# One PSUM bank for two or four groups of a feed-forward's first layer

## The chip, the cores and the metric

The kernel runs on one core of a Trainium2 chip. The metric is device time in microseconds, the median of three runs. Five instruction streams matter: PE (TensorE, matmuls and transposes; PEld is its weight load), DVE (VectorE), ACT (ScalarE), POOL (GpSimd) and SP, which issues nearly all DMAs. Each works through its own queue in order and waits for the others by semaphores.

## The reference

Eight batches of eight heads go through an attention in which each query keeps only its 32 largest scores. The heads are joined to rows of 512, and these go through a feed-forward layer with an ELU.

```python
# q, k, v: (8, 8, 576, 64); w_in: (512, 2048); w_out: (2048, 512)
scores = scale * np.matmul(q, k.transpose(0, 1, 3, 2))
kth = np.partition(scores, -32, axis=-1)[..., -32:-31]
scores = np.where(scores >= kth, scores, -1e9)
attn = np.exp(scores - max) / (sum + 1e-9)
x = (attn @ v) transposed and joined to (4608, 512)
h = x @ w_in
g = np.where(h > 0, h, np.exp(np.minimum(h, 0)) - 1)
out = g @ w_out
```

The kernel computes g as relu(h) + exp(-relu(-h)) - 1. The weights arrive as 64-bit floats, and the kernel turns them into 32-bit floats itself.

## The kernel before

**Attention.** The work is cut into 144 steps. A step is 128 query rows of a pair of heads (or 64 rows of four heads, for the 64 rows that are left of 576). `scores` (L301 on PE, L309 on ACT) forms 2 x 576 scores per row. `select` (L343, L348, L355 on DVE; in the first eight steps `select_row` with L320, L324, L330) finds the 32 largest of each with four rounds of an eight-fold maximum (MAX8) and three replacements between them. `mask` takes the threshold and the maximum on POOL (L368 neg, L370 gap) and masks and exponentiates on ACT (L371, L372). `normalise` forms the reciprocal of the sum and scales the rows on POOL (L382 to L389). `turn` transposes them on PE (L408, tiles eps and scps) with copies on ACT (L409, tile et), and `attend` multiplies by v (L434); ACT copies the result to xT (L461).

**Feed-forward.** Finished rows are gathered in blocks of one, two or three slots of 128 tokens: in the first two batches five blocks of one slot and two of two, and in each later pair of batches three of two slots and one of three. `ffn_pieces(blk)` cuts a block's work into pieces. `hidden(f)`, for f = 0 to 15, is one group: four matmuls (L502) that give 128 hidden units of all tokens of the block in a PSUM tile hps, whose pool `ps_f` has two buffers of one bank (512 fp32 per partition). A fp32 matmul leaves two records in the profile. ACT reads each group twice, relu(-h) to n (L510) and relu(h) to gT (L511). After each second group ACT takes exp(-n) (L513) of both, and a gate is noted. The gate, `close_gates` (L478), is the DVE instruction that forms gT + n - 1. `project` is the second layer, in four parts of four matmuls per slot (L523, tile ops, from the same pool `ps_f`), a copy (L532) and a DMA out.

**Order.** `feed` is called four times a step and takes pieces from the list as their costs and due times allow. It closes a gate at the second feeding place after that in which it was noted. A new pair of groups and `project` may close gates earlier. From step eight on (`tight`) the order of PE, ACT, DVE and POOL is that in which the code names the instructions (`manual_schedule`). In the first eight steps a scheduler orders them. There the 32 weight blocks are also converted, two or three between the rounds of a row (`hook`): three operations on ACT (L170, L171, L172), a clamp on POOL (L173), two on DVE (L180, L183) and an addition on POOL (L187). All hidden groups of the first one-slot block fall into these eight steps too.

Of the kernel before, what the change touches and what calls it, by code (L numbers as in the profile page):

```python
# [8 lines left out]
AF = mybir.ActivationFunctionType  # L9
ALU = mybir.AluOpType  # L10
FP32 = mybir.dt.float32
# [69 lines left out]
def kernel(  # L81
# [9 lines left out]
    nc = tc.nc  # L91
    P = nc.NUM_PARTITIONS
    B, H, S, D = q.shape
    dm, dff = moe_w_in.shape[0], moe_w_in.shape[1] // 2
# [7 lines left out]
    NG = NF // 2  # L102
    T = 3 * P
    KEYS, QUERIES = R, R + S
    scale = 1.0 / float(D) ** 0.5
# [3 lines left out]
    def pool(name, bufs, **kw):  # L109
        return ctx.enter_context(tc.tile_pool(name=name, bufs=bufs, **kw))  # L110
# [12 lines left out]
    ps_f = pool("ps_f", 2, space=PSUM)  # L123
    wide = [ps_sc.tile([P, 2, JP], FP32, tag=f"s{i}", name="scps") for i in range(2)]
    late = {}
    raws = ExitStack()
    early = raws.enter_context(tc.tile_pool(name="early", bufs=1))
    earlyf = raws.enter_context(tc.tile_pool(name="earlyf", bufs=2))
# [326 lines left out]
    def finish(blk, parts, at, cols, src):  # L455
        if blk.xT is None:
            if blk.slots == 1:
                blk.xT = xpool.tile([P, NC, P], FP32, tag="xT", name="xT")
            else:
                blk.xT = late["x"].tile([P, NC, T], FP32, tag="xT", name="xT")  # L460
        nc.scalar.copy(blk.xT[:, at, cols], src)  # L461
        blk.left -= parts
        if blk.left == 0:
            ffn.extend(ffn_pieces(blk))

    gates = []
    place = [0]

    def close_gates(keep=0, upto=None):

        while gates:
            put, group, dst, n = gates[0]
            if put > place[0] - keep if upto is None else group > upto:
                return
            gates.pop(0)
            nc.vector.scalar_tensor_tensor(  # L478
                out=dst, in0=n, scalar=-1.0, in1=dst, op0=ALU.add, op1=ALU.add
            )  # L480

    def ffn_pieces(blk):
        n_tok = blk.slots * P

        def hidden(f):
            if f == 0 and blk.number == 0:
                g = early.tile([P, NF, P], FP32, tag="g", name="gT")
                blk.gT = [g[:, 0:NG], g[:, NG:NF]]
            elif f % NG == 0 and blk.number > 0:
                g = late["g"].tile([P, NG, T], FP32, tag="g", name="gT")  # L490
                blk.gT.append(g[:])
            if f % 2 == 0:
                if len(gates) > 1:
                    close_gates(upto=gates[0][1])
                if blk.number == 0:
                    n = earlyf.tile([P, 2, P], FP32, tag="n", name="n")
                else:
                    n = late["f"].tile([P, 2, T], FP32, tag="n", name="n")
                blk.n = n[:, :, 0:n_tok]
            ps = ps_f.tile([P, dm], FP32, tag="f", name="hps")  # L500
            for i in range(NC):
                nc.tensor.matmul(  # L502
                    ps[:, 0:n_tok],
                    w_in[:, i, f * P : (f + 1) * P],
                    blk.xT[:, i, 0:n_tok],
                    start=(i == 0),
                    stop=(i == NC - 1),
                )
            g = blk.gT[f // NG]
            nc.scalar.activation(blk.n[:, f % 2, :], ps[:, 0:n_tok], AF.Relu, scale=-1.0)  # L510
            nc.scalar.activation(g[:, f % NG, 0:n_tok], ps[:, 0:n_tok], AF.Relu)  # L511
            if f % 2 == 1:
                nc.scalar.activation(blk.n, blk.n, AF.Exp, scale=-1.0)  # L513
                dst = g[:, f % NG - 1 : f % NG + 1, 0:n_tok]
                gates.append((place[0], (blk.number, f - 1), dst, blk.n))

        def project(s, part):
            close_gates(upto=(blk.number, (part + 1) * NF // 4 - 1))
            if part == 0:
                blk.o = ps_f.tile([P, dm], FP32, tag="f", name="ops")  # L520
            step = NF // 4
            for f in range(part * step, (part + 1) * step):
                nc.tensor.matmul(  # L523
                    blk.o[:],
                    blk.gT[f // NG][:, f % NG, s * P : (s + 1) * P],
                    w_out[:, f, :],
                    start=(f == 0),
                    stop=(f == NF - 1),
                )
            if part == 3:  # L530
                o = opool.tile([P, dm], FP32, tag="osb", name="osb")
                nc.scalar.copy(o[:], blk.o[:])  # L532
                for t in blk.tiles[s]:
                    p0 = t.cols.start - s * P
                    nc.sync.dma_start(out[t.rows, :], o[p0 : p0 + t.ql, :])

        part = HIDDEN[blk.slots]
        behind = 2 * NF if blk.number else 0
        return [
            (part, max(behind, NC * (f // 4 + 1)), lambda f=f: hidden(f))  # L540
            for f in range(NF)
        ] + [
            (PROJECT, max(behind, NF + (part + 1) * NF // 4),
             lambda s=s, part=part: project(s, part))
            for s in range(blk.slots)
            for part in range(4)
        ]
# [4 lines left out]
    for b in range(B):  # L552
        if b % 2 == 0:
# [5 lines left out]
            for part in division:  # L559
                blk = Block(len(blocks), len(part))  # L560
# [4 lines left out]
        for qt in range(J + 1):  # L565
# [8 lines left out]
            t = Tile(b, qt, rows, blk, slice(c0, c0 + n))  # L574
# [6 lines left out]
        for qts in order:  # L581
# [3 lines left out]
            for qt in qts:  # L585
                n = len(steps)
# [12 lines left out]
    for b in range(1, B):  # L599
        f = first[b]  # L600
# [137 lines left out]
```

## Time and profile before

| | us |
|---|---|
| median of three runs (1681.44 to 1681.5) | 1681.44 |
| the profiled execution, whole time | 1682.55 |
| the profiled execution, first to last instruction (span) | 1680.8 |
| PE busy | 1604.5 |
| DVE busy | 1534.4 |
| ACT busy | 1167.5 |
| POOL busy | 638.8 |
| mean granted TensorE clock | 0.971 |

The profile is one execution of the program. Times within it count from its first instruction. Line numbers (L502) are those of the kernel file. A row of the groups has engine, operation, tiles (written <- read), shapes and count, then busy time with the mean duration of one in ns, then the idle time of that engine just before and what ended it. A line of waits reads "engine, tile, line <- what it waited for: us in total, times, longest".

### The profile page before, as it was taken

How to read it: one execution, taken by the hardware profiler on the slowest of the kernel's cores; microseconds unless marked ns; L12 is line 12 of the kernel's file. 1: busy time of each engine (PE TensorE's matmuls, PEld its weight loads, DVE VectorE, ACT ScalarE, POOL GpSimd, SP SyncE). 2: the span in 40 equal slices, each digit the busy share in tenths (PEclk: the TensorE clock that was granted, in tenths of full speed). 3: DMA queues.
4: the chain of work that ended last, by engine and by line, in shares of the span. 5: the costliest groups of instructions: out<-in, count | busy, mean ns of one | idle time of the engine just before them, and what ended most of it. 6: DMA issues, size and time to landing. Idle time of an engine off the chain costs nothing.

```text
span 1680.8 us, 26396 instructions
## 1 busy us (share of the span) xinstructions
PE 1604.5 (95%) x8560; PEld 1041.7 (62%) x8560; DVE 1534.4 (91%) x3096; ACT 1167.5 (69%) x2661; POOL 638.8 (38%) x1719
## 2 busy tenths in 40 slices
PE   6767999999999999999999999999999999999999
PEld 4554776667575666656557575756558575755565
DVE  6999999999999999999999999999998999998600
ACT  6776786778776776767768685857758586857531
POOL 3776333433333334434334333333333333332200
PEclk8567999999999999999999999999999999999999
DMA  7441021001200111001200111001100000000000
GB/s 192 134 156 39 16 56 36 7 1 47 52 7 7 29 35 42 1 21 36 49 14 1 36 35 42 1 13 43 43 13 8 21 21 29 7 7 7 7 13 13
DMA packets 101129, 56.22 MB, mean 33 GB/s; under 512 B 84097, under 2 KB 92289, under 8 KB 100993
## 3 DMA queue, kind: packets, MB, share of 16 engines
q1 hardware_dynamic: 99792, 54.26, 11.6%
q8 instruction: 68, 1.11, 0.3%
q14 instruction: 69, 0.56, 0.1%
q10 hardware_dynamic: 1200, 0.30, 0.1%
HBM read 45.09 MB, written 9.44 MB: 32 GB/s over the span
## 4 chain that ended last, share of the span: by engine, by line
PE 59%; DVE 26%; ACT 5%; issue 1%; POOL 1%; ACTq 0%; DVEq 0%; POOLq 0%
PE ops L523 22%; PE hps L502 19%; DVE wk L348 11%; DVE m L355 9%; PE avps L434 7%; PE scps L301 6%; PE eps L408 4%; DVE m L343 3%; DVE gT L478 2%; ACT sc L372 1%; ACT sc L371 1%; PE qkps L271 1%; ACT et L409 1%; PE scps L408 1%; ACT n L510 0%
## 5 line engine op out<-in xcount | busy, mean ns | idle before, releaser
L502 PE MATMUL hps<-xT,w_in 128*128 128x256 f32 (+2 forms) x2432 | 557.4, 378 | 25.9 <-ACT gT L511 23.6
L355 DVE MAX8 m<-wk 128x8 f32<-128x576 f32 x816 | 574.5, 744 | 0.0
L523 PE MATMUL ops<-w_out,gT 128*128 128x512 f32 x1152 | 523.8, 599 | 0.0
L502 PEld LDWEIGHTS hps<-xT,w_in 128*128 128x128 f32 x2432 | 411.5, 195 | 127.4 <-ACT gT L511 34.4
L348 DVE MATCH_REPLACE8 wk<-m,wk 128x576 f32<-128x576 f32 x544 | 399.2, 740 | 0.0
L523 PEld LDWEIGHTS ops<-w_out,gT 128*128 128x128 f32 x1152 | 209.0, 190 | 233.6 <-issue 218.7
L382 POOL TENSOR_SCALAR dene<-den 128x2 f32<-128x2 f32 x144 | 34.8, 242 | 832.9 <-ACT sc L372 832.7
L371 ACT ACTIVATE sc<-sc,neg 128x576 f32<-128x576 f32 x288 | 226.4, 786 | 63.2 <-POOL neg L368 63.0
L372 ACT ACTIVATE sc<-sc,gap 128x576 f32<-128x576 f32 x288 | 223.2, 775 | 25.2
L309 ACT ACTIVATE sc<-scps 128x576 f32<-128x576 f32 x288 | 173.6, 662 | 76.6 <-PE scps L301 76.6
L389 POOL TENSOR_SCALAR sc<-sc,rec 128x576 f32<-128x576 f32 x288 | 219.5, 773 | 15.2 <-POOL rec L387 0.6
L409 ACT COPY et<-eps 128x512 f32<-128x512 f32 x288 | 167.5, 582 | 68.4 <-PE eps L408 68.2
L301 PE MATMUL scps<-kqT 64*128 64x288 f32 (+1 forms) x1280 | 200.5, 439 | 15.1 <-ACT kqT L277 8.3
L348 DVE MATCH_REPLACE8 wk<-m,sc 128x576 f32<-128x576 f32 x272 | 199.6, 740 | 0.0
L408 PEld LDWEIGHTS eps<-ident,sc 128*128 128x128 f32 x1152 | 145.1, 145 | 82.9 <-issue 48.0
L478 DVE SCALAR_TENSOR_TENSOR gT<-n,gT 128x512 f32<-128x512 f32 (+2 forms) x152 | 106.5, 701 | 97.7 <-ACT n L513 97.6
L434 PE MATMUL avps<-et,vT 128*64 128x256 f32 (+2 forms) x2080 | 190.4, 326 | 2.7 <-ACT et L409 2.3
L343 DVE MAX8 m<-sc 128x8 f32<-128x576 f32 x272 | 191.0, 742 | 0.0
L408 PE MATMUL eps<-ident,sc 128*128 128x128 f32 x1152 | 178.1, 281 | 12.9 <-POOL sc L389 11.9
L510 ACT ACTIVATE n<-hps 128x256 f32<-128x256 f32 (+2 forms) x304 | 112.6, 370 | 85.5 <-PE hps L502 75.0
L434 PEld LDWEIGHTS avps<-et,vT 128*64 128x64 f32 x2080 | 123.5, 141 | 73.1 <-issue 24.2
L301 PEld LDWEIGHTS scps<-kqT 64*128 64x128 f32 (+1 forms) x1280 | 107.7, 181 | 83.6 <-issue 44.8
(47 smaller groups left out, 1226.8 us busy)
## 6 DMA issues: line engine op xcount, KB each, us to landing
kin<-in_k_dram SPq DMA_DIRECT2D x64, 128.0 KB, 2.8
raw<-in_moe_w_in_dram SPq DMA_DIRECT2D x16, 512.0 KB, 4.4
vT<-in_v_dram SPq DMA_DIRECT2D x64, 128.0 KB, 2.3
raw<-in_moe_w_out_dram SPq DMA_DIRECT2D x16, 512.0 KB, 3.2
out_dram<-osb SPq DMA_DIRECT2D x32, 256.0 KB, 2.3
qin<-in_q_dram SPq DMA_DIRECT2D x62, 128.0 KB, 2.8
kin<-in_k_dram SPq DMA_DIRECT2D x32, 32.0 KB, 2.5
vT<-in_v_dram SPq DMA_DIRECT2D x64, 16.0 KB, 2.2
```

Source lines behind the costliest of these rows:

```text
L301: nc.tensor.matmul(wide[i][rows, half, 0:HS], kq[part, q0 : q0 + u.t.ql], kq[part, k0 : k0 + HS], start=True, stop=True,)
L343: nc.vector.max(found[i], cur[i])
L348: nc.vector.match_replace(wk[i], found[i], cur[i], TAKEN)
L355: nc.vector.max(found[i], cur[i])
L371: nc.scalar.activation(sc, sc, AF.Prelu, bias=neg[:], alpha=STEEP)
L372: nc.scalar.activation(sc, sc, AF.Exp, bias=gap[:], accum_out=u.den[:, i : i + 1])
L389: nc.gpsimd.tensor_scalar(u.sc[:, i, :], u.sc[:, i, :], rec[:, i : i + 1], 1.0, ALU.mult, ALU.mult)
L408: nc.tensor.transpose(ps[:, c * P : (c + 1) * P], sc[:, c0 : c0 + P], ident[:])
L409: nc.scalar.copy(g.et[:, chunks, u.at, :], ps[:, 0 : n * P].rearrange("p (c q) -> p c q", c=n),)
L434: nc.tensor.matmul(ps[i * D : (i + 1) * D, cols], vt[:, 2 * J + i if c == J else i * J + c, :], w, start=(c == 0), stop=(c == J),)
L502: nc.tensor.matmul(ps[:, 0:n_tok], w_in[:, i, f * P : (f + 1) * P], blk.xT[:, i, 0:n_tok], start=(i == 0), stop=(i == NC - 1),)
L523: nc.tensor.matmul(blk.o[:], blk.gT[f // NG][:, f % NG, s * P : (s + 1) * P], w_out[:, f, :], start=(f == 0), stop=(f == NF - 1),)
```

## The change

The hps tile of a block of one slot now holds four groups (4 x 128 columns), that of two slots two groups (2 x 256), and that of three slots one group, as before (384). ACT reads relu(-h) and relu(h) of the whole bank in one instruction each, after the last of its groups. The unit for which exp and gate are issued is four groups for one slot (512 columns, before 256) and two for two and three slots, as before (512 and 768). The matmuls are the same, and so are the pieces, their costs and their due times. The tile n is addressed without gaps. The line numbers of what follows move by up to eight: the matmul is L506, the reads L516 and L519, exp L521, and the second layer's matmul L531 in the changed file.

```diff
     def ffn_pieces(blk):
         n_tok = blk.slots * P
+        bank = dm // n_tok
+        unit = max(2, bank)
...
-            if f % 2 == 0:
+            if f % unit == 0:
                 if len(gates) > 1:
                     close_gates(upto=gates[0][1])
                 if blk.number == 0:
-                    n = earlyf.tile([P, 2, P], FP32, tag="n", name="n")
+                    n = earlyf.tile([P, 4 * P], FP32, tag="n", name="n")
                 else:
-                    n = late["f"].tile([P, 2, T], FP32, tag="n", name="n")
-                blk.n = n[:, :, 0:n_tok]
-            ps = ps_f.tile([P, dm], FP32, tag="f", name="hps")
+                    n = late["f"].tile([P, 2 * T], FP32, tag="n", name="n")
+                blk.n = n[:, 0 : unit * n_tok].rearrange("p (f t) -> p f t", f=unit)
+            if f % bank == 0:
+                ps = ps_f.tile([P, dm], FP32, tag="f", name="hps")
+                blk.h = ps[:, 0 : bank * n_tok].rearrange("p (f t) -> p f t", f=bank)
             for i in range(NC):
                 nc.tensor.matmul(
-                    ps[:, 0:n_tok],
+                    blk.h[:, f % bank, :],
                     w_in[:, i, f * P : (f + 1) * P],
...
-            g = blk.gT[f // NG]
-            nc.scalar.activation(blk.n[:, f % 2, :], ps[:, 0:n_tok], AF.Relu, scale=-1.0)
-            nc.scalar.activation(g[:, f % NG, 0:n_tok], ps[:, 0:n_tok], AF.Relu)
-            if f % 2 == 1:
+            g, end = blk.gT[f // NG], f % NG + 1
+            if end % bank == 0:
+                n0 = f % unit + 1 - bank
+                nc.scalar.activation(
+                    blk.n[:, n0 : n0 + bank, :], blk.h, AF.Relu, scale=-1.0
+                )
+                nc.scalar.activation(g[:, end - bank : end, 0:n_tok], blk.h, AF.Relu)
+            if end % unit == 0:
                 nc.scalar.activation(blk.n, blk.n, AF.Exp, scale=-1.0)
-                dst = g[:, f % NG - 1 : f % NG + 1, 0:n_tok]
-                gates.append((place[0], (blk.number, f - 1), dst, blk.n))
+                dst = g[:, end - unit : end, 0:n_tok]
+                gates.append((place[0], (blk.number, f + 1 - unit), dst, blk.n))
```

## The prediction

> **What bounds the kernel now.** The page comes first, since it says which engines can be the limit at all.
>
> ```profile
> PE 1604.5 (95%) x8560; PEld 1041.7 (62%) x8560; DVE 1534.4 (91%) x3096; ACT 1167.5 (69%) x2661; POOL 638.8 (38%) x1719
> ```
>
> Two engines are nearly full, PE and DVE. The change takes work mainly from ACT, which is not. So the question is which of the two is the limit where. The busy times by stage answer that (columns: length, then PE, PEld, DVE, ACT, POOL with their instructions, the granted TensorE clock, DMA):
>
> ```profile
> 0.00:42.00 42.00, 26.18 (x111) 17.07 (x112) 28.52 (x59) 26.78 (x53) 14.19 (x42) 0.83 0.70 192
> 42.00:148.00 106.00, 78.19 (x361) 57.48 (x361) 100.28 (x172) 85.38 (x191) 79.86 (x116) 0.65 0.41 131
> 148.00:300.00 152.00, 136.69 (x1091) 99.89 (x1090) 150.50 (x319) 107.26 (x288) 57.81 (x166) 0.98 0.12 30
> 300.00:717.00 417.00, 407.22 (x2291) 273.56 (x2289) 416.34 (x858) 310.45 (x726) 162.17 (x467) 1.00 0.09 23
> 717.00:1600.00 883.00, 879.44 (x4452) 547.20 (x4451) 833.20 (x1685) 618.26 (x1360) 322.76 (x926) 1.00 0.08 22
> 1600.00:1681.00 81.00, 76.73 (x265) 46.51 (x262) 5.54 (x8) 19.33 (x49) 2.04 (x5) 0.99 0.04 13
> ```
>
> From 42 to 717 us DVE lacks only 5.7 + 1.5 + 0.7 us of being full: DVE sets the pace. From 717 us PE lacks 3.6 of 883 us and then 4.3 at the very end: PE sets the pace. The chain of waits, cut to 300 to 717 us, agrees: it is DVE's.
>
> ```profile
> by line: DVE wk L348 42.3%; DVE m L355 35.6%; DVE m L343 12.6%; DVE gT L478 5.7%; issue 2.8%; ACT sc L372 0.4%; ACT sc L371 0.4%; ACT et L409 0.2%; ACT n L513 0.2%; POOL neg L368 0.1%; DVEq L478 0.0%; ACTq L372 0.0%
> ```
>
> Which waits could end? Those of DVE and, apart from them, the one of PE that the change addresses:
>
> ```profile
> DVE gT L478 <- ACT n L513: 97.6, 28, 44.1
> DVE raw L180 <- POOL raw L173: 19.1, 6, 9.7
> ```
>
> ```profile
> PE hps L502 <- ACT gT L511: 23.6, 23, 4.0
> ```
>
> All 23.6 us of the last lie before 717 us (10.0 in 42:148, 9.4 in 148:300, 4.2 in 300:717). There PE has spare time and DVE has none, so ending them gives nothing by itself. Of DVE's 97.6 us only 2.1 lie before 717 us (1.43 at 283 us, 0.66 at 487 us); the rest is DVE waiting for a full PE. Of DVE's 19.1 us on the weight conversion, 5.7 lie in 42:148.
>
> **The change, part by part.** Time is won only where DVE, before 717 us, gets shorter or waits less. A microsecond won there moves everything behind it, because the order of PE's, DVE's and SP's work after 148 us is the same in both programs apart from the gates (L478), whose number falls.
>
> ```profile
> L478 DVE SCALAR_TENSOR_TENSOR gT<-n,gT 128x512 f32<-128x512 f32 x88 | 63.9, 726 | 83.7 <-ACT n L513 83.7
> ...
> L478 DVE SCALAR_TENSOR_TENSOR gT<-n,gT 128x256 f32<-128x256 f32 x40 | 19.0, 476 | 1.4 <-ACT n L513 1.4
> ```
>
> *DVE gates.* The five one-slot blocks had 40 gates of 256 columns and get 20 of 512; those of the other blocks keep number and size. In the chain a 256-wide gate costs 0.32 us and a 512-wide one 0.59. After 148 us: 32 x 0.32 = 10.2 becomes 16 x 0.59 = 9.4, so -0.8. Before 148 us eight gates took 5.3 us, three of them over 1.0; less 0.07 overlap each, 4.7. Four of 512 with one or two held up come to 3.1: -1.6. Here the Trainium skill speaks against: "SBUF — State Buffer", section "Who interferes with whom", says that a DVE instruction with two SBUF inputs contends with a GpSimd instruction that reads SBUF. A gate is one, and a longer one meets POOL more easily. If each of the 20 waited for one 1.3 us POOL addition, the loss would be 26 us and the gates a cost. The rows say otherwise: 476 ns against 400 unhindered is 0.08 per gate, 726 against about 660 is 0.07. The hold-up goes by the gate, not by its length, and there are fewer. I take -2.4 for both stages.
>
> *ACT.* Rows:
>
> ```profile
> L409 ACT COPY et<-eps 128x512 f32<-128x512 f32 x288 | 167.5, 582 | 68.4 <-PE eps L408 68.2
> ...
> L510 ACT ACTIVATE n<-hps 128x256 f32<-128x256 f32 x176 | 67.3, 382 | 46.9 <-PE hps L502 41.2 <-DVE m L355 3.1 <-DVE gT L478 2.6
> L513 ACT ACTIVATE n<-n 128x512 f32<-128x512 f32 x88 | 56.5, 642 | 0.0
> ...
> L510 ACT ACTIVATE n<-hps 128x128 f32<-128x128 f32 x80 | 21.9, 273 | 11.1 <-PE hps L502 6.4 <-DVE gT L478 3.6
> ```
>
> No 512-wide Relu exists; the 512-wide copy out of PSUM (0.58) is the nearest row, and 0.38 to 0.49 from 256 to 384 columns gives 0.59. Two-slot blocks: 352 reads of 0.383 = 135 us become 176 of 0.59 = 104. One-slot: 160 of 0.275 = 44 become 40 of 0.59 = 24, and 40 Exp of 0.423 become 20 of 0.642 (-4). ACT loses 55 us of busy time. None of it counts, as ACT is not the limit. What counts is when the Exp that frees a gate ends. After the last matmul of a two-slot unit there were 0.38 + 0.38 + 0.64 = 1.4 us; now 0.59 + 0.59 + 0.64 = 1.8: 0.4 us later.
>
> The Trainium skill speaks against this part too: "PSUM — Partial Sum Buffer", "Summary: rules for kernel authors", says to read another bank than the one that a matmul writes. So nothing of a bank may be read before its last group is written. That holds the first read back by one two-slot group (8 matmul records x 0.216 = 1.7 us) or three one-slot groups (24 x 0.131 = 3.1 us); 20 one-slot units x 3.1 would be 63 us if DVE stood waiting. In the trace it does not: a gate stands two feeding places behind its last group and waited twice before 717 us. The gate waits for the last group's Exp either way, so the price is 0.4 us at those gates that have no slack. That is the one at 487 us: +0.4. The 1.43 at 283 us stood behind a PE wait for ACT (1.01 us just before) of the kind that two banks of four groups relieve: -1.4 (0 to -1.4). PE's waits for a bank should nearly vanish after 148 us, at no gain.
>
> *The first stage.* Here the order is not written by hand, and the changed program's order differs on all engines. I followed it by hand with the durations of the trace. The stall to explain first, POOL's rows and then DVE's:
>
> ```profile
> 104.29 0.23 POOL L382 TENSOR_SCALAR dene<-den 128x2 f32<-128x2 f32 x1 [1.71 <-ACT sc L372]
> ...
> 108.40 0.75 POOL L389 TENSOR_SCALAR sc<-sc,rec 128x576 f32<-128x576 f32 x1
> 109.24 0.61 POOL L173 TENSOR_SCALAR raw<-raw 128x512 f32<-128x512 f32 x1
> ```
>
> ```profile
> 105.68 0.74 DVE L324 MATCH_REPLACE8 wk<-m,wk 128x576 f32<-128x576 f32 x1
> 109.88 1.51 DVE L180 TENSOR_SCALAR raw<-raw 128x512 uint32<-128x512 uint32 x1 [3.46 <-POOL raw L173]
> ```
>
> The 21st weight's clamp (L173) stands behind a whole normalisation on POOL's queue, and DVE behind the clamp. In the changed order this clamp comes before the normalisation; the 22nd comes behind it. On the other side PE now issues 13 first-layer matmuls in one piece (26 records x 0.26 = 6.8 us, from about 82 to 89 us, and 8 more records), ahead of the transposes (eps) that started at 88.2. ACT's copies of these, and the conversions queued behind them, come later: the 18th by 4 us, the 19th by 2. DVE then stands about 2.1 us at the 19th, where it did not, 1.8 at the 22nd, and 0.45 and 0.9 where it had 1.64 and 0.31: 5.3 in place of 5.7, or -0.4. The conversion that followed the stall at 109.88 ran 1.51 us beside POOL where an unhindered one takes 0.40: -1.1 if it runs free (0 to -1.1; I take -0.8). By the end of this stage: -1.2 besides the gates, with a hand count that may be off by 4 us either way.
>
> *After 717 us* PE's work is unchanged, and it has no idle time to give. 0, bounded by -1 (part of its 3.6 us) and +3 (ACT's longer burst in front of a copy that PE needs). The end is 64 + 128 matmul records back to back: 0.
>
> Sum: gates -2.4, first stage -1.2, wait at 283 us -1.4, wait at 487 us +0.4: -4.6. The profiled span of 1680.8 becomes 1676.2. That execution took 1682.55 in all, and the median of the runs is 1681.44, 0.64 above the span; so about 1676.8.
>
> **The rivals.** A: as summed, 1672 to 1678. B: the first stage gives nothing and the 283 us wait stays: only gates, -2.4 + 0.4, 1679.4. The many reorderings speak for it. It also covers the case in which the change loosens PE's 23.6 us and nothing else, and that in which DVE, 18 times waiting for Exp in 717:1600, hands some of the 0.4 us on. C: the conversion stalls go altogether (-5.7 instead of -0.4): 1671.5. For it speaks the lighter ACT; against it, the normalisation on POOL's queue stays. D, slower: the single-piece bursts on PE. Units two and three of block 0 are issued as 20 and 16 matmuls in one piece, where the first has 13: 3 to 7 x 0.52 = 1.6 to 3.6 us more. If each delays transposes, ACT's in-order queue and a clamp as the first does, DVE stands 3.7 and 5.7 us: +9.4 - 4.6, about 1686.2. It decides from the point where a burst outlasts the roughly 3.4 us that DVE takes from one conversion to the next. Against it: the slow clock (0.65) rises by then, and these bursts stand where fewer conversions queue behind them.
>
> **How the numbers follow.** A 55% (47 faster, 8 same), B 22% (2 faster, 20 same), C 8% (faster), D 15% (13 slower, 2 same). The bound for "same" is 0.2%, or 3.4 us, about what a measurement of this kernel can tell from no change. Faster 0.57, same 0.30, slower 0.13. The range reaches from C less a little, 1670, to the border of D, 1684.
>
> **What would show it.** Right: 20 gates of 512 more and 40 of 256 fewer; ACT near 1112 us busy; Relu at 0.59; PE's wait hps <- ACT under 10 us; DVE's row at 1534 less 3 to 5; the stage after 717 us as long as before. Wrong: new DVE idle before gates in 148:717; more than 8 us of waiting for L173 in 42:148 (D), or next to none (C); PE idle over 8 us after 717.

## The result, and the profile after

The changed kernel takes 1676.97 us, the median of nine runs (1676.32 to 1677.9), where the kernel before took 1681.73 on the same chip: a ratio of 0.997, with a 95% interval of 0.9961 to 0.9978. That is faster, by 4.8 us (3.7 to 6.6). The forecast had said 1676.8. The total is right; two of its terms are off by nearly 2 us each in opposite directions, and that they cancel is luck. The span of the profiled execution fell from 1680.8 to 1675.2, which is 5.6 us and not 4.8: the profiled execution of before (1682.55) lies 0.8 above the median of its runs. A second trace of the changed kernel has a span of 1676.1, 4.7 below.

The page of the changed kernel, busy time by engine:

```profile
PE 1596.1 (95%) x8560; PEld 1034.7 (62%) x8560; DVE 1529.6 (91%) x3076; ACT 1146.1 (68%) x2345; POOL 639.2 (38%) x1719
```

Busy times by stage of the changed kernel (columns as before: length, PE, PEld, DVE, ACT, POOL with their instructions, granted TensorE clock, DMA share, GB/s):

```profile
0.00:42.00 42.00, 24.97 (x112) 16.63 (x113) 28.31 (x59) 26.77 (x53) 14.03 (x42) 0.89 0.68 191
42.00:146.00 104.00, 65.77 (x350) 49.70 (x349) 98.53 (x167) 82.13 (x161) 81.84 (x116) 0.67 0.41 134
146.00:297.00 151.00, 145.61 (x1145) 106.56 (x1144) 150.93 (x312) 108.36 (x228) 60.44 (x173) 0.99 0.12 30
297.00:712.00 415.00, 404.09 (x2246) 269.78 (x2244) 415.00 (x849) 297.73 (x611) 158.58 (x462) 1.00 0.09 23
712.00:1595.00 883.00, 879.56 (x4452) 545.85 (x4453) 831.30 (x1685) 613.86 (x1264) 322.74 (x928) 1.00 0.08 22
1595.00:1676.00 81.00, 76.13 (x261) 46.15 (x259) 5.54 (x8) 17.22 (x33) 1.60 (x3) 0.99 0.04 13
```

From 146 to 712 us DVE is now full to 0.07 us, where it lacked 2.2. ACT has 316 instructions fewer, but only 21 us less busy time.

The waits of DVE, and the wait of PE for a bank, in the changed kernel (engine, tile, line <- what it waited for: us in total, times, longest):

```profile
DVE gT L478 <- ACT n L521: 97.3, 26, 44.5
DVE raw L180 <- POOL raw L173: 19.1, 6, 10.3
```

```profile
PE hps L506 <- ACT gT L519: 0.8, 1, 0.8
```

DVE's two waits for Exp before 717 us are gone, the one at 283 us and the one at 487 us; what is left of them lies in the stage where PE is full, and at the end. PE's wait for a bank fell from 23.6 us to 0.8.

The groups by shape:

```profile
L478 DVE SCALAR_TENSOR_TENSOR gT<-n,gT 128x512 f32<-128x512 f32 x108 | 76.6, 709 | 84.1 <-ACT n L521 84.1
...
L521 ACT ACTIVATE n<-n 128x512 f32<-128x512 f32 x108 | 68.3, 632 | 0.0
L516 ACT ACTIVATE n<-hps 128x512 f32<-128x512 f32 x108 | 63.9, 592 | 43.1 <-PE hps L506 41.7
L519 ACT ACTIVATE gT<-hps 128x512 f32<-128x512 f32 x108 | 63.9, 592 | 0.0
```

A Relu of 512 columns takes 0.592 us, as estimated (0.59), and the gates of 512 are 88 + 20.

**Where the 5.6 us of the span went.** The 144 steps are the same in both programs, so the start of the first MAX8 of each step (L343) can be laid beside that of the other trace. Changed less before:

| DVE's step | at (before), us | difference, us | the stretch that ends here |
|---|---|---|---|
| 9 | 158.59 | -1.01 | the first stage |
| 21 | 280.28 | -2.21 | half as many gates |
| 22 | 292.44 | -4.12 | the wait of 1.43 at 283 us, and a gate |
| 31 | 383.57 | -3.51 | some gates held up by POOL |
| 43 | 508.52 | -4.96 | the wait of 0.66 at 487 us, and two gates |
| 64 | 722.84 | -5.21 | |
| 143 | 1572.60 | -5.60 | the stage of PE |

A single row is good to some tenths of a microsecond only. The second trace of the changed kernel has -0.60 at step 9, -3.70 at step 22, -5.02 at step 43, -4.54 at step 64 and -4.69 at step 143. All kernels with the changed first block lie within 0.9 us of each other at step 9: 0.5 us of it is there at 42 us, and the rest arises up to 82 us, as conversions on DVE take longer or shorter.

### The profile page after: what moved, and what is told of

The parts are those of the page before. It is cut to its first block, busy times and chain, and to the rows that moved or that the text cites. A ratio compares the mean times of both kernels' runs of the same rounds, so it can differ in the third digit from the quotient of the medians.

```text
span 1675.2 us, 26070 instructions
## 1 busy us (share of the span) xinstructions
PE 1596.1 (95%) x8560; PEld 1034.7 (62%) x8560; DVE 1529.6 (91%) x3076; ACT 1146.1 (68%) x2345; POOL 639.2 (38%) x1719
## 3 DMA queue, kind: packets, MB, share of 16 engines
q8 instruction: 68, 1.11, 0.3%
## 4 chain that ended last, share of the span: by engine, by line
PE 59%; DVE 28%; ACT 3%; issue 1%; POOL 0%; ACTq 0%; DVEq 0%
PE ops L531 22%; PE hps L506 19%; DVE wk L348 12%; DVE m L355 10%; PE avps L434 6%; PE scps L301 6%; PE eps L408 4%; DVE m L343 4%; DVE gT L478 2%; PE qkps L271 1%; ACT sc L372 1%; ACT sc L371 1%; PE scps L408 1%; ACT et L409 0%; ACT n L516 0%
## 5 line engine op out<-in xcount | busy, mean ns | idle before, releaser
L506 PE MATMUL hps<-xT,w_in 128*128 128x256 f32 (+2 forms) x2432 | 548.2, 374 | 2.8 <-POOL w_in L187 1.9
L531 PE MATMUL ops<-w_out,gT 128*128 128x512 f32 x1152 | 523.6, 599 | 0.0
L506 PEld LDWEIGHTS hps<-xT,w_in 128*128 128x128 f32 x2432 | 406.9, 193 | 98.7 <-issue 23.6
L531 PEld LDWEIGHTS ops<-w_out,gT 128*128 128x128 f32 x1152 | 209.0, 190 | 233.4 <-issue 220.8
L371 ACT ACTIVATE sc<-sc,neg 128x576 f32<-128x576 f32 x288 | 226.0, 785 | 101.1 <-POOL neg L368 101.0
L372 ACT ACTIVATE sc<-sc,gap 128x576 f32<-128x576 f32 x288 | 223.3, 775 | 25.4 <-ACT sc L371 0.4
L434 PE MATMUL avps<-et,vT 128*64 128x256 f32 (+2 forms) x2080 | 191.8, 325 | 5.9 <-ACT et L409 5.5
L343 DVE MAX8 m<-sc 128x8 f32<-128x576 f32 x272 | 190.5, 739 | 0.0
L478 DVE SCALAR_TENSOR_TENSOR gT<-n,gT 128x512 f32<-128x512 f32 (+1 forms) x132 | 99.9, 757 | 97.3 <-ACT n L521 97.3
L434 PEld LDWEIGHTS avps<-et,vT 128*64 128x64 f32 x2080 | 122.0, 140 | 79.6 <-issue 23.3
L516 ACT ACTIVATE n<-hps 128x512 f32<-128x512 f32 (+1 forms) x156 | 87.3, 560 | 71.4 <-PE hps L506 69.8
```

The lines of the kernel that those rows point to most:

```text
L343: nc.vector.max(found[i], cur[i])
L371: nc.scalar.activation(sc, sc, AF.Prelu, bias=neg[:], alpha=STEEP)
L372: nc.scalar.activation(sc, sc, AF.Exp, bias=gap[:], accum_out=u.den[:, i : i + 1])
L434: nc.tensor.matmul(ps[i * D : (i + 1) * D, cols], vt[:, 2 * J + i if c == J else i * J + c, :], w, start=(c == 0), stop=(c == J),)
L506: nc.tensor.matmul(blk.h[:, f % bank, :], w_in[:, i, f * P : (f + 1) * P], blk.xT[:, i, 0:n_tok], start=(i == 0), stop=(i == NC - 1),)
L531: nc.tensor.matmul(blk.o[:], blk.gT[f // NG][:, f % NG, s * P : (s + 1) * P], w_out[:, f, :], start=(f == 0), stop=(f == NF - 1),)
```

## The experiments

Each edit is shown against the changed kernel. The first four kernels ran on one chip, where before took 1683.02 us; the later ones each have the time of before on their own chip beside them.

**The first block alone.**

```diff
-        bank = dm // n_tok
+        bank = dm // n_tok if blk.number == 0 else 1
```

> Only block 0 (one slot, in the first eight steps, where a scheduler orders the work) gets banks of four groups; all later blocks stay as before. Theory DVE (DVE sets the pace up to about 717 us, so only its gates and waits count): the first stage alone was worth 1.0 to 1.3 us by the starts of DVE's steps, so 1.0 to 1.5 us below before, and step 9 starts where it does in the full change. Rival ACT (the gain comes from 55 us less on ACT or from PE's waits for a bank, wherever they lie): block 0 has 16 of 304 groups and 10 of PE's 23.6 us of waits, so 0.3 by ACT's share or about 2 by PE's waits.

Measured: 1682.07, ratio 0.9995 [0.9986, 1.0003]. In the table of steps it is 1.27 us ahead at step 9 and 1.45 at step 143: nothing is added or lost later. All that the first stage gives is about 1 us, which the runs alone do not tell from nothing (the interval includes 1).

**All blocks but the first.**

```diff
-        bank = dm // n_tok
+        bank = dm // n_tok if blk.number > 0 else 1
```

> All blocks but block 0 get the wide banks; the first eight steps stay as before. Theory DVE: what the full change wins from step 9 on, 4.6 us by the starts of the steps and the span, so 3.5 to 5 below before; first stage unchanged. Rival (the first stage's new order is what won): under 1.5.

Measured: 1678.52, ratio 0.9972 [0.9962, 0.9983]. At step 22 it is 3.75 ahead, at step 43 5.04, at step 143 5.09. Its first stage has the order of before, and yet it is 0.8 us ahead from 72 us on: 0.2 by its start, the rest because single conversions on DVE took other times (one 1.05 us in place of 1.76). So some 4.3 us come from the later blocks. Together with the 1.45 of the first block that is 5.7, about the change's 5.6, but two gates show how loose such a sum is. In the changed kernel, DVE's gates at two places (start, duration):

```profile
335.54 0.99 DVE L478 SCALAR_TENSOR_TENSOR gT<-n,gT 128x512 f32<-128x512 f32 x1
...
356.95 1.11 DVE L478 SCALAR_TENSOR_TENSOR gT<-n,gT 128x512 f32<-128x512 f32 x1
```

and the second of them in the kernel with all blocks but the first:

```profile
357.36 0.68 DVE L478 SCALAR_TENSOR_TENSOR gT<-n,gT 128x512 f32<-128x512 f32 x1
```

What POOL does at that time differs. First the changed kernel, then the other:

```profile
356.79 1.90 POOL L389 TENSOR_SCALAR sc<-sc,rec 128x576 f32<-128x576 f32 x2
```

```profile
358.78 0.75 POOL L389 TENSOR_SCALAR sc<-sc,rec 128x576 f32<-128x576 f32 x1
```

The gate of 1.11 us runs beside POOL's scaling of a row; the gate of 0.68 us is over before that scaling starts.

**Wider gates, banks as before.**

```diff
-        bank = dm // n_tok
-        unit = max(2, bank)
+        bank = 1
+        unit = max(2, dm // n_tok)
```

> One-slot blocks take exp and gate for four groups (20 gates of 512 columns in place of 40 of 256), but each group keeps its own bank and its own two reads; two-slot and three-slot blocks as before. Theory DVE: the gates' 1.1 us after 148 us and about 1.5 before, less some new waits since PE still waits for banks: 1 to 2.5 below before; DVE's waits at 283 and 487 us (2.1 together) stay. Rival ACT: ACT gets only 4 us lighter, PE's bank waits stay near 24 us, so no gain beyond 0.5.

Measured: 1679.45, ratio 0.9985 [0.9976, 0.9994]. The runs scatter from 1678.69 to 1682.93: the medians lie 3.6 us apart, the ratio stands for 2.5, and the trace is of one of the quicker runs. It is 0.11 ahead at step 9, 3.20 at step 22 and 3.33 at step 143. PE's and DVE's waits in this kernel, over the whole of it for PE and from 146 to 717 us for DVE:

```profile
PE hps L506 <- ACT gT L519: 22.4, 26, 4.0
```

```profile
DVE gT L478 <- ACT n L521: 0.3, 1, 0.3
```

PE waits for its banks as long as before, and still DVE's wait of 1.43 us at 283 us is gone. The expectation that it would stay was wrong. That wait does not need PE's waits to end; a gate that covers four groups, at another place, ends it too.

**Banks and reads changed, gates and exp of two groups as before.**

```diff
-            if f % unit == 0:
-                if len(gates) > 1:
-                    close_gates(upto=gates[0][1])
+            if f % unit == 0:
+                if len(gates) > unit // 2:
+                    close_gates(upto=gates[-1 - unit // 2][1])
...
-                nc.scalar.activation(blk.n, blk.n, AF.Exp, scale=-1.0)
-                dst = g[:, end - unit : end, 0:n_tok]
-                gates.append((place[0], (blk.number, f + 1 - unit), dst, blk.n))
+                for j in range(0, unit, 2):
+                    n, e = blk.n[:, j : j + 2, :], end - unit + j
+                    nc.scalar.activation(n, n, AF.Exp, scale=-1.0)
+                    dst = g[:, e : e + 2, 0:n_tok]
+                    gates.append((place[0], (blk.number, f + 1 - unit + j), dst, n))
```

> Banks and reads as in the full change, but exp and gate stay at two groups (40 gates of 256 columns for the one-slot blocks). Theory DVE: no gain from gates, but the two waits of DVE at 283 and 487 us go (2.1) and the gates held up near 500 us run free (about 0.8): 2 to 3.5 below before. Rival ACT: all of the gain, 4.5 to 5, since ACT's reads and PE's bank waits are those of the full change.

Measured: 1678.78, ratio 0.9975 [0.9966, 0.9985]; by the medians 4.2 below before, more than the 2 to 3.5 expected. It is 3.25 ahead at step 22 and 3.72 at step 143. PE's wait for a bank is 0.8 us, and DVE has no wait at all from 146 to 717 us. Gates alone and banks alone each take the 1.43 us away. So that wait is counted twice when their gains are added: 3.3 + 3.7 - 1.4 = 5.6. That this meets the full change's 5.6 to the tenth is chance, since each figure is of one trace, and the wait at 487 us is shared in part too (0.3 of its 0.66 is left with gates alone).

**Which blocks carry it.** Two kernels divide the change by the size of the block.

```diff
-        bank = dm // n_tok
+        bank = dm // n_tok if blk.slots == 2 else 1
```

> Only two-slot blocks get banks of two groups; one-slot blocks stay at one group, with gates of 256 columns. No gate changes in number or size. Theory DVE: the wait at 487 us goes (0.66) and gates held up by POOL near 500 us may run free (up to 0.8), nothing else before 717 us: 0.5 to 1.5 below before, with DVE's wait at 283 us (1.4) still there. Rival ACT: this is where ACT gets 31 of its 55 us: 2.5 to 3 below before.

Measured: 1682.83 beside 1682.21, ratio 1.0007 [0.9998, 1.0016]. By the rows of before and after, these blocks take 31 us out of ACT's sum of durations, and nothing comes of it. It is 1.46 us ahead at step 43, as expected, but 0.93 at step 64 and 0.03 at step 143. Of what it gives back, 0.5 is gates that take longer again between steps 43 and 64; what takes the other 0.9, in the stage where PE is full, stays open.

```diff
-        bank = dm // n_tok
+        bank = dm // n_tok if blk.slots == 1 else 1
```

> Only one-slot blocks get banks of four groups and gates of four; two-slot blocks as before. Theory DVE: the full change's gain up to step 41, 3.5 us, less or more 0.6 by how DVE's gates meet POOL; the wait near 487 us stays: 3 to 4 below before. Rival ACT: 24 of 55 us, about 2.2 below before.

Measured: 1676.67 beside 1682.21, ratio 0.9968 [0.9955, 0.998]. The one-slot blocks carry the whole gain, and more than the 3 to 4 us expected, since the wait near 487 us went as well. On another chip, beside the full change:

> The full change once more, beside the others on one chip: 1677 within 1 us by every theory. It is the base from which the extra operation's price and the one-slot part's share are read.

> Only the blocks of one slot share a bank (four groups), once more beside the full change. If the two-slot blocks' single pass gives nothing, this is within 0.7 us of the full change (before: 0.3 us below it on another chip). If the 31 us of reads that it saves on ACT count for anything, the full change is at least 1 us faster than this.

Measured: the full change 1677.30, the one-slot part alone 1676.78, with before at 1682.43 (ratios 0.997 and 0.9966). They cannot be told apart. On ACT the one-slot kernel is busy for 1156.6 us, 10 more than the full change, and that costs nothing.

**Is ACT's time free?** The prediction had said that none of it counts. The doubled read:

```diff
-                nc.scalar.activation(
-                    blk.n[:, n0 : n0 + bank, :], blk.h, AF.Relu, scale=-1.0
-                )
+                for _ in range(2 if blk.slots == 2 else 1):
+                    nc.scalar.activation(
+                        blk.n[:, n0 : n0 + bank, :], blk.h, AF.Relu, scale=-1.0
+                    )
```

> The full change, but in two-slot blocks relu(-h) is read from the bank twice, one after the other (88 more instructions of 0.59 us: ACT gets 52 of its 55 us back, 43 at the rate of instructions back to back). The result is the same. Theory DVE (ACT's time counts for nothing, only DVE's gates and waits before 717 us): within 1.5 us of the full change, about 5 below before; Exp ends 0.5 us later, so DVE's wait near 487 us may come back with up to 0.7. Rival ACT: 4 to 5 us of the gain go, so about as before.

Measured: 1691.63 beside 1682.21, ratio 1.006 [1.0046, 1.0073]: some 14 us over the full change, for 50 us more of ACT. Neither theory had foreseen that. Against the trace of the full change 6.6 us are lost by step 64 and 7.8 from there to step 143. Before 717 us DVE waits again for Exp (this kernel, 146 to 717 us):

```profile
DVE gT L478 <- ACT n L522: 4.4, 4, 1.9
```

The next kernel has the same extra work at another place.

```diff
             g, end = blk.gT[f // NG], f % NG + 1
+            if blk.slots == 2 and f % 2 == 0:
+                nc.scalar.activation(blk.n, blk.xT[:, 0:2, 0:n_tok], AF.Relu)
             if end % bank == 0:
```

> The full change, and at the first group of every two-slot unit one more ACT operation (a 512-wide Relu of finished rows, from SBUF, written to n and overwritten later): 88 x about 0.5 us = 44 to 52 us more on ACT, as much as the doubled read had added, but away from the end of the unit, where the gate's Exp waits. If the doubled read cost 14 us because it lengthened what stands between a unit's last matmul and its Exp (the delay theory), most of that does not come here: 0 to 5 us over the full change, 1677 to 1682. If it cost 14 us because ACT has no time to give at all (the load theory), it comes here too: about +14, near 1691. A figure between, +5 to +10, would say that both count.

Measured: 1682.92, ratio to before 0.9999 [0.999, 1.0008]: 5.6 over the full change of the same chip. That is neither theory's figure but the case between: work on ACT costs in either place, and at the end of the unit, in front of the Exp, about twice as much for each microsecond of ACT. Here 2.4 us are lost by step 64, of which DVE waits 1.4 for an Exp, and 3.5 from there to step 143. The added operation itself waits 0.6 us for a gate to free its tile, so that is not the price. What PE waits for is seen on the weight loads of `attend` (L434, PEld). First the changed kernel, then the extra operation between, then the doubled read:

```profile
L434 PEld LDWEIGHTS avps<-et,vT 128*64 128x64 f32 x2080 | 122.0, 140 | 79.6 <-issue 23.3 <-ACT et L409 15.4 <-ACT kqT L277 2.5
```

```profile
L434 PEld LDWEIGHTS avps<-et,vT 128*64 128x64 f32 x2080 | 122.6, 141 | 82.2 <-issue 23.9 <-ACT et L409 18.4 <-ACT kqT L277 2.5
```

```profile
L434 PEld LDWEIGHTS avps<-et,vT 128*64 128x64 f32 x2080 | 124.9, 142 | 88.2 <-ACT et L409 24.2 <-issue 22.2 <-PE scps L301 2.7
```

They stand 15.4, 18.4 and 24.2 us for ACT's copy et. That the copy sits behind the longer burst in ACT's queue is the likely reading; it was not followed case by case. PE's row hides this. The stretch from 717 to 1600 us, in the same order:

```profile
717.00:1600.00 883.00, 879.85 (x4442) 545.58 (x4441) 826.30 (x1674) 613.10 (x1261) 321.48 (x923) 1.00 0.08 22
```

```profile
717.00:1600.00 883.00, 879.54 (x4439) 544.66 (x4436) 828.31 (x1679) 634.38 (x1308) 323.50 (x922) 1.00 0.08 22
```

```profile
717.00:1600.00 883.00, 879.43 (x4445) 545.34 (x4445) 833.80 (x1687) 640.52 (x1312) 319.49 (x923) 1.00 0.08 22
```

PE is busy for 879.4 to 879.9 of 883 us in all three, though by the starts of DVE's steps 64 and 143 the second loses 3.5 us against the first in this stretch and the third 7.8. The weight loads' waits for et there are 1.9, 3.9 and 5.7 us. They name 2.0 of the 3.5 and 3.8 of the 7.8; the rest is not assigned.

Last, the mirror of the doubled read: ACT made lighter at the same place.

```diff
-                nc.scalar.activation(blk.n, blk.n, AF.Exp, scale=-1.0)
+                e = blk.n[:, 0:1, 0:P] if blk.slots == 2 else blk.n
+                nc.scalar.activation(e, e, AF.Exp, scale=-1.0)
```

> The full change, but in the two-slot blocks the Exp covers only the first 128 of its 512 columns (the rest of n goes into the gate without it): 88 Exp of about 0.3 us in place of 0.64, so some 30 us less on ACT, at the end of the unit. It is the mirror of the doubled read. If ACT's time there has a price in both directions (0.16 to 0.3 us per us), 1677.3 falls by 5 to 9, to 1668 to 1672. If the full change already lies below the point from which a late Exp costs anything, it stays within 1 us of the full change.

Measured: 1676.88 beside 1683.0, ratio 0.9964 [0.995, 0.9978]. ACT is busy for 1120.6 us, 26 less than in the full change, and the time is the same. So the price of ACT's time has a bend. From 1121 to 1157 us of ACT (the one-slot kernel) it is nothing, which fits that the two-slot blocks' single pass brings nothing. At 1188 it comes to 0.13 us per us of ACT added to the full change (5.6 for 42) where the work lies between, at 1196 to 0.29 (14.4 for 50) where it stands before the Exp. Where between 1157 and 1188 the bend lies was not measured, and the kernels differ in where the work stands as well as in how much it is.

## Why the prediction was right, and where it was not

**The bound.** Right where it was used: DVE's pace up to 717 us, and in it gates and waits, give 5.2 of the 5.6 us. "PE's bank waits would end at no gain" holds in size: they fell by 22.8 us for a gain of a fourth of that at most. As a general statement it fails: earlier matmuls are one of two ways in which the wait at 487 us ends.

**Gates.** Predicted -2.4. Before 148 us the eight took 5.5 us (the prediction had read 5.3) and the four take 3.8 (0.67, 1.00, 1.38, 0.77): -1.7, for -1.6. From step 9 to 31 the change is 2.5 us ahead, of which 1.43 is the wait, so -1.1 is left for gates, for -0.8. The rule on two SBUF inputs against POOL was weighed rightly: of the sixteen new gates after 148 us, fourteen take 0.67 or 0.68 us and two, held up by POOL, 0.99 and 1.11; the mean of all 512-wide gates is 709 ns, not above the 726 of before. The one of 1.38 us in the first stage shows that the rule has a price, but not one that goes with the number of columns.

**The first stage apart from gates.** Predicted -1.2; this is the term that failed most. DVE's stalls on the conversion, in the changed kernel:

```profile
99.16 1.53 DVE L180 TENSOR_SCALAR raw<-raw 128x512 uint32<-128x512 uint32 x1 [1.14 <-POOL raw L173]
...
111.83 0.83 DVE L180 TENSOR_SCALAR raw<-raw 128x512 uint32<-128x512 uint32 x1 [1.69 <-POOL raw L173]
...
129.89 0.43 DVE L180 TENSOR_SCALAR raw<-raw 128x512 uint32<-128x512 uint32 x1 [1.36 <-POOL raw L173]
...
134.64 1.49 DVE L180 TENSOR_SCALAR raw<-raw 128x512 uint32<-128x512 uint32 x1 [1.28 <-POOL raw L173]
```

The hand count had 2.1, 1.8, 0.45 and 0.9: four stalls, as it turned out, and the sum 5.3 against 5.5 measured. What did not come is the 0.8 us for the conversion that "runs free". It does at the old place (0.41 us at 107.80), but the one behind the new stall at 99 us takes 1.53 us, as the old one at 109.88 did (1.51). The two conversion operations together take 43.2 us from 62 us on, where they took 42.8. A held-up conversion moved and did not end. The stage gave about -1 in all, with -1.7 of gates in it, so the remainder is +0.7 in place of -1.2, of which up to 0.9 may be the spread between traces at step 9. The burst that was feared (rival D) is there:

```profile
81.87 6.53 PE L506 MATMUL hps<-xT,w_in 128*128 128x128 f32 x34
88.56 0.66 PE L408 MATMUL eps<-ident,sc 128*128 128x128 f32 x4 [0.16 <-POOL sc L389]
```

But it did not do what was feared. All 34 records took the 6.5 us that the hand count had given to 26, and the transposes behind them started at 88.56, only 0.35 us later than before (88.21). The stall at 99 us came as forecast, though not along the forecast path of transposes, copies and a late clamp. The clamp on POOL that DVE waits for there, in the changed kernel and in the kernel before:

```profile
98.51 0.61 POOL L173 TENSOR_SCALAR raw<-raw 128x512 f32<-128x512 f32 x1 [2.37 <-ACT raw L170]
```

```profile
98.66 0.61 POOL L173 TENSOR_SCALAR raw<-raw 128x512 f32<-128x512 f32 x1 [0.85 <-ACT raw L170]
```

```profile
100.14 0.52 DVE L180 TENSOR_SCALAR raw<-raw 128x512 uint32<-128x512 uint32 x1
```

The clamp is not late but 0.15 us early. DVE is ready for it at 98.02 and not, as before (third row), at 100.14, and so it stands where it did not. Part of the time that DVE gains in this stage is lost again in waiting for a conversion that comes no sooner. The later, longer bursts brought no stall above 1.7 us, where D had 3.7 and 5.7.

**The wait at 283 us.** Predicted -1.4; the wait of 1.43 us is gone. The reason given, PE's wait for a bank just before, is not needed: with PE's waits left as they were, wider gates end it too.

**The wait at 487 us.** Predicted +0.4, measured -1.4 with the two gates behind it (-0.66 the wait alone). This is the step with the wrong sign. The prediction counted what ACT does after the last matmul of the unit (1.4 us, then 1.8) and left out what is queued on ACT before it. ACT of the kernel before, start, duration and the idle time before it:

```profile
481.81 0.39 ACT L510 ACTIVATE n<-hps 128x256 f32<-128x256 f32 x1 [1.54 <-PE hps L502]
482.09 0.38 ACT L511 ACTIVATE gT<-hps 128x256 f32<-128x256 f32 x1
482.36 0.78 ACT L371 ACTIVATE sc<-sc,neg 128x576 f32<-128x576 f32 x1
...
486.27 0.36 ACT L510 ACTIVATE n<-hps 128x256 f32<-128x256 f32 x1
486.54 0.38 ACT L511 ACTIVATE gT<-hps 128x256 f32<-128x256 f32 x1
486.80 0.63 ACT L513 ACTIVATE n<-n 128x512 f32<-128x512 f32 x1
```

ACT stands 1.54 us before the read of the unit's first group. The masks of the step (L371, L372) stand behind that read, and the read of the second group, whose matmuls had ended at 484.05, behind the masks. The same place in the kernel with two-slot blocks alone, where PE's matmuls run at the same time to 0.04 us:

```profile
480.21 0.78 ACT L371 ACTIVATE sc<-sc,neg 128x576 f32<-128x576 f32 x1
...
484.59 0.58 ACT L516 ACTIVATE n<-hps 128x512 f32<-128x512 f32 x1
485.07 0.59 ACT L519 ACTIVATE gT<-hps 128x512 f32<-128x512 f32 x1
485.55 0.63 ACT L521 ACTIVATE n<-n 128x512 f32<-128x512 f32 x1
```

There is no read of the first group to wait for, so the masks start 2.1 us earlier, and the Exp starts at 485.55 and not at 486.80. The single pass lengthens the tail and takes a wait out of the queue ahead of it. In the full change, PE's freed banks add to this: its matmuls of that unit start at 472.33 where they had started at 479.78, 7.45 us earlier, while DVE is only 3.51 earlier. Either would have been enough: the kernel with one-slot blocks alone, which reads this unit as before, has no wait there either. The two gates of before that start at 498.32 and 507.48 took longer (0.90 and 1.12 us, the second beside POOL's scaling of a row) and do not now (0.67 and 0.66), by timing that nothing in the prediction could have told.

**After 717 us.** Predicted 0; measured -0.4, within what one row of that table is worth (-0.15 in the second trace). It was right at this load only: the doubled read shows that PE, full as its row looks, hands on what ACT adds.

**ACT's busy time.** Predicted near 1112, measured 1146. The durations of the rows did fall by about 55 us. But two reads in a row start 0.28 us apart where each is 0.39 long (481.81 and 482.09 above), and the page counts the common 0.1 once. For 512 columns they start 0.48 apart (484.59 and 485.07). Two reads of 256 columns therefore cost ACT about 0.55 us, and the one of 512 in their place 0.48: a merge saves 0.07, not the 0.18 that 0.77 less 0.59 would give. Busy time fell by 21 us; the other 34 had been overlap.

## What to carry to other kernels

Cost an operation on an in-order queue by the distance between starts, not by its row's duration, and when reads are merged, look also at the wait that disappears from the queue ahead of the read, not only at the tail behind it. That an engine is not the limit means that making it lighter gains nothing (26 us less of ACT, no gain), not that adding to it is free (42 us more cost 5.6): before adding, ask which short copy behind it feeds the engine that is full, and put the work away from the operation that others wait for. And parts that each end the same wait must not be summed: here gates alone gave 3.3 us, banks alone 3.7, both 5.6.

## What the runs showed of the hardware

A PE row at 879 of 883 us is no proof that PE has nothing to give or lose: kernels 7.8 us apart in that stretch show the same row, and about half of the difference is found on the weight loads' waits. The Trainium skill ("Perfetto Trace Analysis", section "Identifying the Most-Contended Engine") says that matmul occupancy is no good measure of how close a kernel is to the roofline, because pipelined matmuls look smaller in the trace. This case bears out the caution from another side: the row looks full, and still does not tell 3.5 or 7.8 us lost. A 512-wide gate takes 0.66 to 1.4 us, and the long one that was looked into ran beside POOL, so that kernels with the same instructions can differ by half a microsecond per gate. Of changes below 1 us, the table of steps can tell the place, but a second trace is needed to trust the size.
